# Turning the tail rows of K and Q, and the LayerNorm rows, by DMA transposes instead of TensorE products

## The chip, the cores and the metric

The kernel runs on one core of a Trainium2 chip. The metric is device time in microseconds of one execution, lower is better. "Span" is the time from the first to the last instruction of one profiled execution.

## What is computed

The reference is the forward and backward pass of a small transformer block; all inputs are bf16, and it returns the output and eleven gradients. What matters here is the forward attention, which is recurrent over segments of 32 tokens:

```python
mem = mem0                                   # 8 rows of width 512
for s in range(64):                          # 2048 tokens in segments of 32
    xs = h[:, s*32:(s+1)*32, :]              # h = layernorm(x) * (1 + ca) + sa
    hcat = concat([mem, xs])                 # 40 rows
    q, k, v = hcat @ Wq, hcat @ Wk, hcat @ Wv    # 32 heads of width 128
    p = softmax(where(mask, q @ k.T * scale, -1e9))
    o = (p @ v) @ Wo                         # 40 x 512
    mem = o[:8]                              # carried to the next segment
    out.append(o[8:])
```

After it come the gated feed-forward block and then the gradients of everything.

## The kernel before

The phases run one after the other. The forward attention (`phase2`) takes about the first 960 us of the span. It loops over 64 steps, one for each segment. Four steps make a group, since 4 x 32 = 128 rows of x are one tile; I call them first to fourth step (`s4` = 0 to 3 in the code).

**The rows of a step.** Of the 40 rows of a segment only the 8 memory rows depend on the step before. The kernel splits them as 32 + 8: `hT` holds, as columns, the 8 memory rows and the first 24 rows of x, and the last 8 rows of x of all four segments of a group (the tail rows, tile `hb`) are projected together, one group ahead, in pieces that fill TensorE where a step has to wait. K and Q of the tail rows are collected as rows in the tiles `RBk` and `RBq` and must be turned into columns, `b_colsk` and `b_colsq` (two buffers each), from which GpSimd copies eight columns per head into the tiles `kT` and `qT` at the end of every step (`tails_in`).

**One step on TensorE** goes: K's and Q's projections of the 32 rows (`pass_ps`, L257); V's projection in three pieces (L659), between them the turning of K's and Q's rows (`turn_ps`, L829); the scores (`st_ps`, L839), which ScalarE takes through Exp into `ET` (one buffer, L841); the denominators (`or_ps`, L845) and the products with V (`or_ps`, L865); VectorE inverts the denominators (`rden`, L850) and scales into `Ost` (one buffer, L889; ScalarE does a third of it at L886); `Ost` is turned (`tps`, L857) and copied into `OT` (one buffer); the output projection (`at_ps`, L223); its folding (`at_ft`), from which the next step's memory columns come.

**Where the changed work stands.** In the third step, behind the products with V, TensorE turns K's tail rows in eight products (`turn_b`, L623); in the fourth step it does the same with Q's. They stand just ahead of the turning of `Ost`. After the output projection ScalarE and VectorE each copy one half out of PSUM (`evac_turned`). In the fourth step, ahead of the last products with V, TensorE turns the LayerNorm rows `h1` of the tile two groups ahead (`turn` of `p1_tile`, four products into `p1tp`, L420); ScalarE copies them to `hx`, and GpSimd copies the tail columns from `hx` to `hb`.

**SP's queue.** SP issues nearly all DMAs of the loop in program order. For each step: K's and Q's rows to DRAM (`KST`, `QST`, L594 and L595), a DMA transpose `VTr<-Vst` (L954) and a DMA transpose `Pst<-ET` (L962), each of 128 x 1408 values, that is 11 blocks of 128 x 128, then the stores of `Ost` (`OSR`, L997) and `OT` (L1010), and in the next step those of `VTr` (`VT`, L1040) and `Pst` (`PS`, L1041). Ahead of the last one GpSimd multiplies `Pst` by the inverted denominators (`norm`, L1038). At the end of the second and third steps the tail rows go out too, in six DMAs (L599, L602). GpSimd issues the copies of V's tail rows (`Vst<-RBv`, L794) and some small stores.

**What sets the order.** The order of every engine is the order of the program: `pin` adds a dependency from each instruction of the loop to the one before it on its engine. Waits between engines come from the tile framework, by tiles and buffers.

Of the kernel before, what the change touches and what calls it, by code (L numbers as in the profile page):

```python
# [9 lines left out]
AF = mybir.ActivationFunctionType  # L10
# [30 lines left out]
class K:  # L41
# [334 lines left out]
    def phase1_setup(self, ctx, psum_tile_fn):  # L376
        nc, tc, cfg, io = self.nc, self.tc, self.cfg, self.io
        D, DC, NT = cfg.D, cfg.DC, cfg.NT
        x_rows = io["A_x"].rearrange("o s d -> (o s) d")
        p1 = ctx.enter_context(tc.tile_pool(name="p1", bufs=1))  # L380
        p1w = ctx.enter_context(tc.tile_pool(name="p1w", bufs=2))
        ca1_bc = self.ca1_bc = p1.tile([128, D], F32, name="ca1_bc")
        sa_bc = self.sa_bc = p1.tile([128, D], F32, name="sa_bc")
        mhalf = p1.tile([128, 1], F32, name="mhalf1")
        nc.gpsimd.memset(mhalf[:], -0.5)
        nseg = 128 // cfg.T

        def p1_tile(j):

            st = {}  # L390

            def load():
                st["x0"] = p1w.tile([128, D], BF16, name="x0_1", bufs=1)
                nc.sync.dma_start(st["x0"][:], x_rows[j * 128:(j + 1) * 128, :])

            def stats():
                bs = p1w.tile([128, 6], F32, name="st1")
                nc.vector.bn_stats(bs[:], st["x0"][:])
                mv = p1w.tile([128, 2], F32, name="mv1")
                nc.vector.bn_aggr(mv[:], bs[:])  # L400
                ve = p1w.tile([128, 1], F32, name="ve1")
                nc.vector.tensor_scalar_add(ve[:], mv[:, 1:2], EPS)
                rstd = p1w.tile([128, 1], F32, name="rstd1")
                nc.gpsimd.tensor_tensor(rstd[:], ve[:], mhalf[:], op=ALU.pow)
                st.update(mv=mv, rstd=rstd)

            def scale():
                xh = st["xh"] = p1w.tile([128, D], F32, name="xh", bufs=1)
                nc.vector.tensor_scalar(xh[:], st["x0"][:], st["mv"][:, 0:1], st["rstd"][:, 0:1], op0=ALU.subtract, op1=ALU.mult)
                nc.vector.tensor_tensor(xh[:], xh[:], ca1_bc[:], op=ALU.mult)  # L410

            def shift():
                h1 = st["h1"] = p1w.tile([128, D], BF16, name="h1", bufs=1)
                nc.vector.tensor_tensor(h1[:], st["xh"][:], sa_bc[:], op=ALU.add)
                nc.gpsimd.dma_start(self.H1ROWS[j * 128:(j + 1) * 128, :], h1[:])

            def turn():
                tp = psum_tile_fn()
                for c in range(DC):
                    nc.tensor.transpose(tp[:, c, :], st["h1"][:, c * 128:(c + 1) * 128], self.ident[:])  # L420
                hx = p1w.tile([128, DC, 128], BF16, name="hx", bufs=3)
                nc.scalar.activation(hx[:], tp[:, 0:DC, :], AF.Copy)
                hb = p1w.tile([128, DC, nseg, 8], BF16, name="hb", bufs=2)
                nc.gpsimd.tensor_copy(hb[:], hx[:].rearrange("p c (s t) -> p c s t", t=cfg.T)[:, :, :, 24:cfg.T])
                return hx, hb

            return load, stats, scale, shift, turn

        return p1_tile

# [8 lines left out]
    def phase2(self):  # L439
        nc, tc, cfg, io = self.nc, self.tc, self.cfg, self.io  # L440
        D, DC, H, E, L, M, T, G, NS = cfg.D, cfg.DC, cfg.H, cfg.E, cfg.L, cfg.M, cfg.T, cfg.G, cfg.NS
# [13 lines left out]
        with ExitStack() as ctx:  # L455
# [38 lines left out]
            P1_AHEAD = 2  # L494
            NT = cfg.NT
            nseg_t = 128 // T
            hxs = {}

            def p1(j, k=None):
                if j < NT:  # L500
                    if j not in p1s:
                        p1s[j] = p1_tile(j)
                    for i in (range(1, 5) if k is None else [k]):
                        r = p1s[j][i]()
                        if r is not None:
                            hxs[j] = r
# [101 lines left out]
            def b_pieces(t):  # L608

                bt = btails[t] = {}  # L610
                RBt = RB

                def proj_b(x, a, n, eng):
                    hb = hxs[t][1]
                    self.col_pass(psp, Ws[x], 0, lambda c: hb[:, c, :, :].rearrange("p s q -> p (s q)"), RBt[x], eng, steps=(a, n))
                    if a + n == 8:
                        rows_out(RBt[x], DR[x], t * nseg_t, nseg_t)

                def turn_b(x):
                    bt[x] = btp.tile([128, 8, 128], BF16, name="b_cols" + x)  # L620
                    tp = psp.tile([128, 8, 128], BF16, name="turn_ps", tag="p")
                    for i in range(8):
                        nc.tensor.transpose(tp[:, i, :], RBt[x][:, i * 128:(i + 1) * 128], self.ident[:, :])  # L623

                    def f():
                        for hf in range(2):
                            self.evac(("act", "dve")[hf], bt[x][:, 4 * hf:4 * hf + 4, :], tp[:, 4 * hf:4 * hf + 4, :])

                    evacs.append(f)

                P = lambda x, a, n, eng: (lambda: proj_b(x, a, n, eng))
                T_ = lambda x: (lambda: turn_b(x))
                return {(0, "f1"): [P("k", 0, 4, "dve")], (1, "f1"): [P("k", 4, 4, "dve")], (1, "f2"): [P("q", 0, 2, "act")],
                        (2, "turn"): [T_("k")], (2, "f1"): [P("q", 2, 4, "dve")], (2, "f2"): [P("q", 6, 2, "act")],
                        (3, "turn"): [T_("q")]}

            evacs = []

            def evac_turned():
                while evacs:  # L640
                    evacs.pop(0)()

            first = b_pieces(0)
            firsts = {x: [first[k][0] for k in ks] + [evac_turned]
                      for x, ks in (("k", ((0, "f1"), (1, "f1"), (2, "turn"))),
                                    ("q", ((1, "f2"), (2, "f1"), (2, "f2"), (3, "turn"))))}
            slots = {}

            VCH = ((0, 4), (4, 4), (8, 3))
# [20 lines left out]
            def hb_rows(t):  # L670
                return lambda c: hxs[t][1][:, c, :, :].rearrange("p s q -> p (s q)")
# [10 lines left out]
            def v_chunk(s, k):  # L682

                t, s4 = s // nseg_t, s % nseg_t
                a, n = VCH[k]
                tails_of = VTAILS.get((s4, k), ()) if t + 1 < NT else ()
                ps = psp.tile([128, 512], F32, name="pass_ps", tag="p")
                hT = get_ht(s)
                for c in range(DC):
                    for j in range(3):  # L690
                        v_mm(ps, j, c, hT[:, c, :], j, a, n)
                    for of in tails_of:
                        v_mm(ps, 3, c, hb_rows(t + 1)(c), *of)
                if k > 0:
                    v_evac(("dve", "act")[k - 1], Vsts[s % 2], ps, a, n)
                for hl, ta, tn, o in tails_of:
                    self.evac(("act", "dve")[k], RBv[(t + 1) % 2][32 * hl:32 * hl + 32, ta * E:(ta + tn) * E],
                              ps[96:128, o * E:(o + tn) * E])
                if k == 0:
                    v_evac("dve", Vsts[s % 2], ps, a, n)  # L700

            def fill(s4, where):
                for f in slots.pop((s4, where), []):
                    f()
# [81 lines left out]
            def tails_in(xs, s):  # L786
                for x in xs:
                    to_heads("pool", XT[x], btails[s // nseg_t][x][:], 0, 8, 8, 8 * (s % nseg_t))
# [15 lines left out]
            for s in range(NS):  # L804
                s4 = s % nseg_t
# [124 lines left out]
                    v_tails(0)  # L930
                if s == NS - 1:
                    first_tile[4]()
                v_chunk(s, 0)
                turns()
                v_chunk(s, 1)
# [30 lines left out]
                ost(0, or0, "dve")  # L966
                ost(1, or1, "act")
                den(2, or2)
                if s4 == 3:
                    p1(s // nseg_t + P1_AHEAD, 4)  # L970
                early = s4 == 0 and len(self.later) > 1
                if early:
                    self.pop_later()
# [3 lines left out]
                pv(2, or2)  # L977
                recip(2, 3, or2)
                ost(2, or2, "dve")
                fill(s4, "turn")  # L980
                if s == NS - 1:
                    turn_v(2)
                if more and s4 < 2:
# [21 lines left out]
                    first_tile[6]()  # L1005
                if s + 1 < NS:
                    tails_in("kq", s + 1)
                parts = self.split_pair(sb2, at_ps, "at")
                tail.collect(s4, [OT])
                nc.sync.dma_start(self.OT[s], gl3(OT))  # L1010
# [15 lines left out]
                if s + 1 in mod_at:  # L1026
                    load, products = self.mod_rest(psp, sb2, mod_at.index(s + 1))
# [1371 lines left out]
```

## Time and profile before

| what | value |
|---|---|
| median of 3 runs | 3001.38 us (2998.03, 3001.38, 3002.90) |
| span of the profiled execution | 2991.0 us, 105890 instructions |
| mean granted TensorE clock | 0.996 |
| DMA engines busy, mean GB/s | 0.86 and 216 over one group of the loop, 400.00 to 457.15 us |
| DMA traffic of the whole run | 703.05 MB, of it 486.09 MB on SP's queue |

Of the profiled execution the page gives only its span; the median of the runs is 10.4 us more, which is taken for what lies around it. In the views, PE is TensorE, PEld its weight loads, DVE VectorE, ACT ScalarE, POOL GpSimd and SP the engine whose queue issues most DMAs. A row of a timeline gives start, duration, engine, line, operation, output and input tiles and, in brackets, how long the engine was idle before it and what ended that. Matmuls are pipelined: the duration of one includes its way through the array, and several overlap, so rows are compared by their starts. A row of the table by windows gives busy time by engine with the number of instructions, then the granted clock, the mean busy share of the 16 DMA engines (packets are counted where they start, and may overlap, so that it can be above 1) and GB/s.

### The profile page before, as it was taken

The numbers are of one execution on the slowest core, as the hardware profiler recorded it, in microseconds if no ns is written. First come the engines' busy times: TensorE is split into PE (matmuls) and PEld (weight loads), VectorE is DVE, ScalarE is ACT, GpSimd is POOL, SyncE is SP. The second block draws the span as 40 slices with busy tenths as digits, with TensorE's granted clock in tenths as the row PEclk, the third lists the DMA queues.
The fourth block names the chain that finished last, engine by engine and source line by source line (L and its number), as shares of the span: only waits on it lengthen the run. The fifth ranks groups of instructions, "written<-read, shape, count | busy, mean of one in ns | idle before, by whom it ended". The sixth has DMA issues, their size and how long they took to land.

```text
span 2991.0 us, 105890 instructions
## 1 busy us (share of the span) xinstructions
PE 2932.8 (98%) x43975; PEld 1839.9 (62%) x44049; DVE 1612.4 (54%) x3679; ACT 1271.8 (43%) x3057; POOL 1197.2 (40%) x2456
## 2 busy tenths in 40 slices
PE   6999999999999999999999999999999999999999
PEld 3666666666665544445677777777777754445454
DVE  5566656666655788833456665566566532222230
ACT  2555555555555533312355555555555520011111
POOL 2454555555545222221344444444444422333321
PEclk8999999999999999999999999999999999999999
DMA  9898888889889899998699999999999997766574
GB/s 310 222 223 211 214 217 217 213 214 215 217 218 277 211 230 226 229 290 278 200 251 251 251 253 243 250 250 250 255 255 250 254 281 245 242 207 214 178 245 144
DMA packets 836438, 703.05 MB, mean 235 GB/s; under 512 B 536643, under 2 KB 708851, under 8 KB 835061
## 3 DMA queue, kind: packets, MB, share of 16 engines
q1 hardware_dynamic: 710756, 486.09, 65.5%
q0 software_dynamic: 54640, 148.90, 15.7%
q10 hardware_dynamic: 70560, 61.28, 6.5%
q8 instruction: 347, 5.69, 0.8%
q14 instruction: 135, 1.10, 0.1%
HBM read 294.99 MB, written 276.35 MB: 191 GB/s over the span
## 4 chain that ended last, share of the span: by engine, by line
PE 87%; issue 5%; DMA 3%; DVE 2%; POOL 1%; ACT 1%; SPq 1%; DVEq 0%; POOLq 0%; ACTq 0%
PE pass_ps L257 14%; PE gps L2180 9%; PE dh_ps L215 8%; PE pass_ps L659 5%; PE g_ps L1810 5%; PE gps5o L2195 4%; PE dhq_ps L223 4%; PE at_ps L223 4%; PE mm L1291 3%; PE dh_tps L215 3%; PE gps L1470 3%; PE turn_ps L829 2%; PE mm L1266 2%; PE mm L1251 1%; PE tps L1727 1%
## 5 line engine op out<-in xcount | busy, mean ns | idle before, releaser
L2180 PE MATMUL gps<-rows,hrows 128*128 128x512 bf16 (+2 forms) x2125 | 415.6, 355 | 1.8
L2180 PEld LDWEIGHTS <-hrows 128*128 128x128 bf16 x2160 | 211.3, 98 | 204.5
L61 ACT ACTIVATE ot<-gps 128x512 bf16<-128x512 f32 (+3 forms) x75 | 41.3, 550 | 362.2 <-PE gps L2180 229.1
L1855 POOL COPY dOst<-RAd 96x512 bf16<-96x512 bf16 x128 | 75.3, 613 | 297.8 <-DVE RAd L63 297.8
L1038 POOL TENSOR_TENSOR Pst<-Pst,rden 120x1408 bf16<-120x1408 bf16 x63 | 159.9, 2538 | 77.8 <-issue 49.6
L659 PE MATMUL pass_ps<-Wv,hT 128*32 128x512 bf16 (+2 forms) x2304 | 187.2, 358 | 0.0
L63 DVE CAST ot<-gps 128x512 bf16<-128x512 f32 (+3 forms) x76 | 48.1, 633 | 247.0 <-PE gps L2180 169.9
L2184 POOL DMA_DIRECT2D out_dram<-ot x108 | 81.5, 755 | 249.1 <-DVE ot L63 141.9
L257 PEld LDWEIGHTS <-hT 128*32 128x32 bf16 x4096 | 114.8, 97 | 103.9 <-issue 5.7
L63 DVE CAST Vst<-pass_ps 96x512 bf16<-96x512 f32 x128 | 87.3, 682 | 107.0 <-ACT RBv L61 98.5
L215 PE MATMUL dh_ps<-WvT,dVT 128*32 128x512 bf16 x2048 | 133.3, 380 | 1.7
L659 PE MATMUL pass_ps<-Wv,hb 128*32 128x512 bf16 (+2 forms) x636 | 128.7, 353 | 0.0
L257 PE MATMUL pass_ps<-Wq,hT 128*32 128x512 bf16 x2048 | 123.9, 383 | 4.8 <-DMA Wq<-in_A_Wq_dram 4.8
L257 PE MATMUL pass_ps<-Wk,hT 128*32 128x512 bf16 x2048 | 123.2, 382 | 2.5 <-POOL hT L549 1.1
L223 PE MATMUL at_ps<-Wo,OT 128*32 128x256 bf16 x4096 | 123.9, 273 | 0.7 <-DMA Wo<-in_A_Wo_dram 0.6
L257 PE MATMUL pass_ps<-WoT,dyT 128*32 128x256 bf16 (+1 forms) x3072 | 122.5, 308 | 0.9 <-ACT dyT L1936 0.9
L223 PE MATMUL dhq_ps<-WqT,dQT 128*32 128x256 bf16 x4096 | 122.9, 273 | 0.0
L215 PE MATMUL dh_ps<-WkT,dKT 128*32 128x512 bf16 x2048 | 122.3, 380 | 0.0
L794 POOL DMA_DIRECT2D Vst<-RBv x192 | 99.9, 526 | 55.6 <-ACT ET L841 34.4
L2195 PE MATMUL gps5o<-WoT,rows 128*128 128x512 bf16 x548 | 120.6, 379 | 1.0 <-DMA rows<-OSR 0.4
L223 PEld LDWEIGHTS <-dQT 128*32 128x32 bf16 x4096 | 109.7, 97 | 15.8
L315 DVE TENSOR_TENSOR dST<-dh_ps,dST 128x512 bf16<-128x512 f32 x64 | 44.3, 692 | 129.9 <-ACT dST L314 129.9
(471 smaller groups left out, 6991.2 us busy)
## 6 DMA issues: line engine op xcount, KB each, us to landing
OSR<-Ost SPq DMA_DIRECT2D x64, 352.0 KB
OT<-OT SPq DMA_DIRECT2D x64, 352.0 KB
PS<-Pst SPq DMA_DIRECT2D x64, 352.0 KB
Pst_l<-PS SPq DMA_DIRECT2D x64, 352.0 KB
OT_l<-OT SPq DMA_DIRECT2D x64, 352.0 KB
DVR<-rows_x POOLq DMA_DIRECT2D x64, 352.0 KB, 6.3
DKR<-rows_x POOLq DMA_DIRECT2D x64, 352.0 KB, 5.7
DQR<-rows_x POOLq DMA_DIRECT2D x64, 352.0 KB, 3.4
```

What stands on the lines that cost most here:

```text
L63: return nc.vector.tensor_copy(out, in_)
L215: self.nc.tensor.matmul(ps[32 * j:32 * j + 32, :], lhsT=lhsT, rhs=w, start=(n < 4), stop=(n >= total - 4), tile_position=(0, 32 * j))
L223: nc.tensor.matmul(ps[32 * j:32 * j + 32, :], lhsT=x[k], rhs=w[k][:, 256 * d:256 * d + 256], start=(n == 0), stop=(n == total - 1), tile_p ...
L257: self.nc.tensor.matmul(ps[32 * j:32 * j + 32, :], lhsT=lhs(c), rhs=rhs, start=(c == 0), stop=(c == DC - 1), tile_position=(0, 32 * j))
L659: nc.tensor.matmul(ps[32 * j:32 * j + 32, o * E:(o + n) * E], lhsT=lhsT, rhs=wc[:, 3 * a + hl:3 * (a + n - 1) + hl + 1:3, :], start=(c == ...
L794: nc.gpsimd.dma_start(Vst[96 + 8 * j:104 + 8 * j, :], rb[32 * j + o:32 * j + o + 8, :])
L1038: nc.gpsimd.tensor_tensor(Pst[0:120, :, :], Pst[0:120, :, :], rden[:, :].unsqueeze(2).to_broadcast([120, G, 128]), op=ALU.mult)
L1291: nc.tensor.matmul(hp[:], lhsT=xT[:, fc, :], rhs=wT[:, fc, :], start=(n == 0), stop=(n == 2 * FC - 1))
L1470: nc.tensor.matmul(ps[:], lhsT=h2r[:, j, c * 128:(c + 1) * 128], rhs=xr[:, j, :], start=(j == 0), stop=(j == NT - 1))
L1810: nc.tensor.matmul(ps[:, j, 0:w], lhsT=lh[:, g * GW:(g + 1) * GW], rhs=rh[:, g * GW:g * GW + w], start=True, stop=True)
L2180: nc.tensor.matmul(ps[:, 0:ng * E], lhsT=hrows[:, tp_, c * 128:(c + 1) * 128], rhs=rows[:, tp_, 0:ng * E], start=(tp_ == 0), stop=(tp_ == ...
L2195: nc.tensor.matmul(pss[gg][:], lhsT=rows[:, t, gg * E:(gg + 1) * E], rhs=dyrows[:, t, :], start=(n == 0), stop=(n == NTP - 1))
```

## The change

From the second group on (`t > 0`) K's and Q's tail rows are turned by one DMA transpose each (128 x 1024 values, eight blocks), issued by SP ahead of `VTr<-Vst` in the third and fourth steps, instead of eight products and two copies. From the third tile on (`j >= 2`) the LayerNorm rows are turned by one DMA transpose (128 x 512 values, four blocks), issued at the same place of the fourth step, instead of four products and a copy; GpSimd's copy of the tail columns moves behind the output projection (`ends`). The first group, and the first two tiles, stay as they were.

```diff
             def turn():
-                tp = psum_tile_fn()
-                for c in range(DC):
-                    nc.tensor.transpose(tp[:, c, :], st["h1"][:, c * 128:(c + 1) * 128], self.ident[:])
                 hx = p1w.tile([128, DC, 128], BF16, name="hx", bufs=3)
-                nc.scalar.activation(hx[:], tp[:, 0:DC, :], AF.Copy)
+                if j < 2:
+                    tp = psum_tile_fn()
+                    for c in range(DC):
+                        nc.tensor.transpose(tp[:, c, :], st["h1"][:, c * 128:(c + 1) * 128], self.ident[:])
+                    nc.scalar.activation(hx[:], tp[:, 0:DC, :], AF.Copy)
+                else:
+                    nc.sync.dma_start(hx[:], st["h1"][:], transpose=True)
                 hb = p1w.tile([128, DC, nseg, 8], BF16, name="hb", bufs=2)
-                nc.gpsimd.tensor_copy(hb[:], hx[:].rearrange("p c (s t) -> p c s t", t=cfg.T)[:, :, :, 24:cfg.T])
+                st.update(hx=hx, hb=hb)
+                if j < 2:
+                    ends()
                 return hx, hb
 
-            return load, stats, scale, shift, turn
+            def ends():
+                nc.gpsimd.tensor_copy(st["hb"][:], st["hx"][:].rearrange("p c (s t) -> p c s t", t=cfg.T)[:, :, :, 24:cfg.T])
+
+            return load, stats, scale, shift, turn, ends
...
                 def turn_b(x):
                     bt[x] = btp.tile([128, 8, 128], BF16, name="b_cols" + x)
+                    if t > 0:
+                        nc.sync.dma_start(bt[x][:], RBt[x][:, 0:1024], transpose=True)
+                        return
                     tp = psp.tile([128, 8, 128], BF16, name="turn_ps", tag="p")
...
-                        (2, "turn"): [T_("k")], (2, "f1"): [P("q", 2, 4, "dve")], (2, "f2"): [P("q", 6, 2, "act")],
-                        (3, "turn"): [T_("q")]}
+                        (2, "rows"): [T_("k")], (2, "f1"): [P("q", 2, 4, "dve")], (2, "f2"): [P("q", 6, 2, "act")],
+                        (3, "rows"): [T_("q")]}
...
                 if s == NS - 1:
                     first_tile[4]()
+                fill(s4, "rows")
+                if s4 == 3:
+                    p1(s // nseg_t + P1_AHEAD, 4)
                 v_chunk(s, 0)
                 turns()
...
                 den(2, or2)
-                if s4 == 3:
-                    p1(s // nseg_t + P1_AHEAD, 4)
...
                 ost(2, or2, "dve")
-                fill(s4, "turn")
...
                 if s + 1 < NS:
                     tails_in("kq", s + 1)
+                if s4 == 3:
+                    p1(s // nseg_t + P1_AHEAD, 5)
                 parts = self.split_pair(sb2, at_ps, "at")
```

More of the change, by code (lines that the diff above doesn't have):

```diff
@@ L644, in phase2 @@
             firsts = {x: [first[k][0] for k in ks] + [evac_turned]
-                      for x, ks in (("k", ((0, "f1"), (1, "f1"), (2, "turn"))),
-                                    ("q", ((1, "f2"), (2, "f1"), (2, "f2"), (3, "turn"))))}
+                      for x, ks in (("k", ((0, "f1"), (1, "f1"), (2, "rows"))),
+                                    ("q", ((1, "f2"), (2, "f1"), (2, "f2"), (3, "rows"))))}
             slots = {}
```

## The prediction

> **What bounds the kernel now.** I read the page, then the attention loop's stretch: one group of four steps in the engines' table, TensorE and VectorE by timeline, SP's queue, the waits.
>
> ```profile
> PE 2932.8 (98%) x43975; PEld 1839.9 (62%) x44049; DVE 1612.4 (54%) x3679; ACT 1271.8 (43%) x3057; POOL 1197.2 (40%) x2456
> ```
>
> ```profile
> core 0: us, PE busy (x) PEld busy (x) DVE busy (x) ACT busy (x) POOL busy (x), PEclk, DMA share, GB/s
> 404.00:406.00 2.00, 2.00 (x44) 1.04 (x40) 0.80 (x2) 0.52 (x2) 1.47 (x3) 1.00 1.01 393
> 456.50:461.30 4.80, 4.66 (x113) 3.50 (x115) 3.40 (x9) 1.78 (x6) 2.68 (x9) 1.00 1.19 150
> 400.00:457.15 57.15, 57.01 (x1136) 38.30 (x1135) 34.95 (x84) 33.12 (x89) 29.63 (x60) 1.00 0.86 216
> ```
>
> The last row is one group, 57.15 us: TensorE busy 57.01 at full clock, DMA engines 0.86. Two engines are near their limit and the change moves work from the first to the second. But the busy time of a pipelined matmul covers the wait of its successor, so 57.01 doesn't say that removed matmuls shorten the group. Ask what starts the next thing that cannot move. For the removed products it is the output projection (at_ps). Here is its approach in a third step (K's turn is there) and in the last group's third step, which has no tail rows and so no turn:
>
> ```profile
> 425.63 0.37 PE L845 MATMUL or_ps<-ones,ET 128*128 128x1 bf16 x8
> 426.65 0.33 PE L865 MATMUL or_ps<-Vst,ET 128*128 128x128 bf16 x3
> 426.81 0.61 PE L623 MATMUL turn_ps<-ident,RBk 128*128 128x128 bf16 x8
> 427.26 0.38 PE L857 MATMUL tps<-ident,Ost 120*128 120x120 bf16 x4
> 428.20 1.06 PE L223 MATMUL at_ps<-Wo,OT 128*32 128x256 bf16 x32
> ...
> 940.22 0.37 PE L845 MATMUL or_ps<-ones,ET 128*128 128x1 bf16 x8
> 941.74 0.38 PE L857 MATMUL tps<-ident,Ost 120*128 120x120 bf16 x4 [0.18 <-DVE Ost L889]
> 942.75 1.49 PE L223 MATMUL at_ps<-Wo,OT 128*32 128x256 bf16 x48
> ```
>
> From the denominators to at_ps it is 428.20 - 425.63 = 2.57 us with the turn and 942.75 - 940.22 = 2.53 without. VectorE shows why:
>
> ```profile
> 426.11 0.21 DVE L850 RECIPROCAL rden<-or_ps 120x8 f32<-120x8 f32 x1 [0.33 <-PE or_ps L845]
> 426.41 0.69 DVE L889 TENSOR_TENSOR Ost<-or_ps,rden 120x512 bf16<-120x512 f32 x1
> 427.02 0.18 DVE L850 RECIPROCAL rden<-or_ps 120x3 f32<-120x3 f32 x1
> 427.23 0.56 DVE L889 TENSOR_TENSOR Ost<-or_ps,rden 120x384 bf16<-120x384 f32 x1
> 427.73 0.41 DVE L63 COPY OT<-tps 128x480 bf16<-128x480 bf16 x1
> ```
>
> Five instructions back to back, then at_ps 0.06 us after the last. The turn (426.81 to 427.26) lies wholly under them.
>
> **What the change removes.** The instruction order shows 15 x 8 products for K, 15 x 8 for Q, 14 x 4 for LayerNorm, and their copies; otherwise TensorE, VectorE and ScalarE keep their order. The chain of work gives these products 0.45, 0.45 and 0.24 us, so 15 x 0.90 + 14 x 0.24 = 16.9 us of TensorE time. On the path is less:
> - K's turn: 2.57 - 2.53 = 0.04 us, 15 times: 0.6. Q's turn stands in the same place of the fourth step; I give it the same 0.6.
> - LayerNorm's four products stand ahead of the last or_ps products, for which the second reciprocal waits, so they delay VectorE's chain. A fourth step with them (439.84 to 442.62) takes 2.78 us; that of the last group but one, which has Q's turn but no LayerNorm products (897.53 to 900.07), 2.54. 14 x 0.24 = 3.4.
> - The copies (ScalarE 603 and VectorE 425 ns for K and for Q, ScalarE 615 for hx) lie ahead of at_hi, before which ScalarE still idles 0.68 us for at_ps in the fourth step: nothing on the path.
>
> Sum of gains: 0.6 + 0.6 + 3.4 = 4.6 us.
>
> **What it adds.** 44 transposes on SP, an in-order queue. No transpose of these sizes is in the trace; the nearest are those of 11 blocks:
>
> ```profile
> L954 SPq DMA_TRANSPOSE VTr<-Vst x63: 1281/1782/3419, 53.2 to 941.6; - x63
> L962 SPq DMA_TRANSPOSE Pst<-ET x63: 1288/1834/3164, 56.7 to 943.0; - x63
> ```
>
> Per block 0.12, 0.16 and 0.31 us. Eight blocks (K, Q) then hold SP for 0.9, 1.3 or 2.5 us, four (hx) for 0.5, 0.65 or 1.2, plus 0.1 between issues. I take the median rows, the same kind of instruction from the same queue. On the DMA engines the window 456.50:461.30, nearly all transposes, moved 150 GB/s at a share of 1.19, that is 126 GB/s of full engine time; plain rows (404:406) 393/1.01 = 389. The added 256 + 256 + 128 KB per group cost 655/126 = 5.2 us by the first and 1.7 by the second; I take 5.2. Idle in the group: 0.14 x 57.15 = 8.0. So the engines hold, at a share of about 0.95.
>
> [...]
>
> **Who waits.** SP around the two places:
>
> ```profile
> 426.10 0.43 SPq L595 DMA_DIRECT2D QST<-RA0q  x1
> 426.76 1.91 SPq L954 DMA_TRANSPOSE VTr<-Vst  x1
> 431.36 0.40 SPq L1010 DMA_DIRECT2D OT<-OT  x1
> 432.45 0.63 SPq L599 DMA_DIRECT2D QST<-RBq  x1
> ...
> 440.72 0.42 SPq L595 DMA_DIRECT2D QST<-RA1q  x1
> 441.37 1.70 SPq L954 DMA_TRANSPOSE VTr<-Vst  x1
> 443.17 1.86 SPq L962 DMA_TRANSPOSE Pst<-ET  x1
> ```
>
> K's transpose goes ahead of 426.76, where SP has hardly a gap: VTr, Pst, OSR and OT issue 1.4 us later. The gap before 432.45 (0.69 us) takes half back. In the fourth step Q's and hx's go ahead of 441.37: 1.3 + 0.65 + 0.2. So VTr, Pst, OSR and OT issue there 0.7 + 2.15 = 2.9 us late, up to 1.9 + 3.9 = 5.8 with the longest issues. Neither new transpose waits on fresh data: the rows and h1 are made in the step before. Who needs what is late:
> - ET has one buffer: the next step's Exp (ScalarE, 453.55) waits until Pst's transpose has read it. Before, it had landed at 448.25, when GpSimd's norm starts on it: 5.3 us of cover. Over the loop's fourth steps the same difference is 3.9 to 6.0.
> - Ost and OT, one buffer each, are stored behind Pst and rewritten at 455.3 and 456.9; issued at 445.1 and 446.5, a store of 352 KB takes 352 x 1.024/389 = 0.9 us, so they have over 5 us too.
> - norm (2.54 us) moves with Pst to about 451, and the PS store, K's and Q's row stores and VTr behind it on SP; SP's gaps before the PS store and VTr (1.6 and 1.5 us) and the wait of 3.9 us in the step after take it back. Row buffers are double.
> - GpSimd: the copies of Q's columns wait for Q's transpose and hb for hx's, with ao_tail, hT, norm and the three Vst stores queued behind. Their readers are the next step's scores (453) or later; GpSimd waited 2.5 us ahead of norm and 5.7 behind the Vst stores.
>
> So in most groups nothing late reaches TensorE. For the tightest boundaries (about 4 us of cover) I add 1 us in all. Forecast: 3001.4 - 4.6 + 1.0 = 2997.8. The profiled span is 2991.0, 10.4 below the median; I keep that difference for what lies around, so a span of 2987.4. Its own range is 2994 to 3003.
>
> **Rivals.**
> 1. All removed TensorE time comes out: 3001.4 - 16.9 = 2984.5. For: TensorE 57.01 of 57.15. Against: 2.57 against 2.53. It would need VectorE's chain to start earlier, and nothing ahead of it is removed.
> 2. Slower: Pst's transpose lands after the next Exp is ready, and TensorE waits for ET. It decides once SP and the DMA engines put it back more than 5.3 - 0.3 = 5.0 us; with the longest issues 5.8, so 0.8 per group, 15 x 0.8 = 12: 3001.4 - 4.6 + 12 = 3008.8, and 3016 where delays reach 6.3. For: the fourth step's SP has no gap from 432.45 on, and the share goes to 0.95. Against: needs maxima three times running.
> 3. The DMA engines become the bound: were the cost twice 5.2, 10.4 - 8.0 = 2.4 us per group are over, 15 x 2.4 = 36: 3033. Against: the window's rate already holds the transposes' stalls. [...]
>
> **How the numbers follow.** Forecast 0.60, rival 1 0.10, rival 2 0.25, rival 3 0.05. A measurement of this kernel can tell about 0.2%, 6 us: below 2995.4 is faster (rival 1 and 0.03 of the forecast's), above 3007.4 slower (rivals 2 and 3, but for 0.05 of rival 2 that stays below). So 0.13, 0.62, 0.25. The range of 8 in 10 leaves out rival 1, rival 3 and the upper end of rival 2: 2989 to 3014.
>
> **What would show it.** Right: denominators to at_ps stays near 2.53 in third and fourth steps; VTr in fourth steps issues 2 to 4 us later against the step; no wait of Exp on a DMA. Wrong: third steps shorter by 0.4 (rival 1); ScalarE or TensorE waiting on Pst<-ET, or groups over 57.15 (rival 2); a DMA share of 1 with SP late in every step (rival 3).

## The result and the profile after

The change made the kernel slower: 3045.55 us, the median of four runs (3041.03 to 3045.70), against 3002.14 us before, a ratio of 1.0154 with a 95% interval of 1.0141 to 1.0167. The forecast was 2997.8 us, with 2989 to 3014 as range.

Of every execution since the prediction both the time and the span are known, and the time is the span plus 1.7 to 2.2 us, mostly 1.8. So of the 10.4 us hardly 2 lie around the span. By that the profiled execution before took some 2992.8 us, 9.3 below the median; that after took 3041.0 us, 4.5 below its median. The two profiles differ by 48.2 us, of which 33.1 lie in 14 groups of the attention loop: from at_ps of the fourth step to at_ps of the 60th it was 800.85 us (99.22 to 900.07), and is 833.93. The rest is 3.8 ahead of that, 5.7 in the last four steps and 5.7 behind the loop. The same stretches outside the loop sum to between 2193 and 2210 us in the other variants (2190 before, 2205 after), so I explain only the loop's 33.1 us, 2.36 per group (57.20 to 59.57).

First the busy time on the page, then the loop in the table by windows:

```profile
PE 2940.0 (97%) x43679; PEld 1831.0 (60%) x43753; DVE 1596.9 (53%) x3649; ACT 1250.7 (41%) x3013; POOL 1193.7 (39%) x2456
```

```profile
core 0: us, PE busy (x) PEld busy (x) DVE busy (x) ACT busy (x) POOL busy (x), PEclk, DMA share, GB/s
103.04:936.97 833.93, 800.47 (x15552) 526.63 (x15550) 472.74 (x1125) 442.77 (x1191) 411.18 (x835) 0.99 0.91 217
```

TensorE is busy 800.47 of 833.93 us; before it was 797.23 of 800.85. So it now stands idle for 33 us instead of 4, with 275 matmuls less to do. The clock fell from 1.00 to 0.99. The DMA engines' share is 0.91, not 0.95, and no bound.

Now the approach to at_ps in TensorE's timeline, a third step and then a fourth:

```profile
442.85 0.37 PE L856 MATMUL or_ps<-ones,ET 128*128 128x1 bf16 x8
445.38 1.93 PE L223 MATMUL at_ps<-Wo,OT 128*32 128x256 bf16 x64
...
457.03 0.35 PE L856 MATMUL or_ps<-ones,ET 128*128 128x1 bf16 x8
459.60 1.60 PE L223 MATMUL at_ps<-Wo,OT 128*32 128x256 bf16 x52
```

From the denominators it is 2.53 and 2.57 us, where it was 2.57 and 2.78: this step of the prediction held (medians over 14 groups: 2.56 to 2.53 in third steps, 2.77 to 2.51 in fourth steps). TensorE waits elsewhere. The waits between 100 and 900 us (engine, line, tile waited for: us in total, times, longest):

```profile
POOL qT L65 <- DMA b_colsq<-RBq: 78.6, 14, 7.7
ACT ET L852 <- DMA Pst<-ET: 19.0, 12, 2.7
PE pass_ps L670 <- POOL hb L433: 14.2, 12, 2.2
PE or_ps L856 <- ACT ET L852: 10.8, 19, 1.8
```

14.2 + 10.8 = 25.0 us, where no wait of TensorE in the same groups before was longer than 0.7 us. Four of these waits were also followed by 3.4 us at half clock (last section), by estimate 1.7 us lost each (half of 3.4): 6.8. Together 31.8, nearly the 33.1. Where the lateness comes from is seen in SP's queue, here from a third step into a fourth:

```profile
271.72 1.46 SPq L976 DMA_TRANSPOSE Pst<-ET  x1
...
276.68 1.83 SPq L610 DMA_DIRECT2D QST<-RBq  x3
278.56 0.46 SPq L1053 DMA_DIRECT2D VT<-VTr  x1
279.13 0.36 SPq L1054 DMA_DIRECT2D PS<-Pst  x1
...
282.67 1.51 SPq L603 DMA_DIRECT2D QST<-RA1q  x1
284.23 1.27 SPq L630 DMA_TRANSPOSE b_colsq<-RBq  x1
285.55 1.27 SPq L425 DMA_TRANSPOSE hx<-h  x1
287.05 1.38 SPq L968 DMA_TRANSPOSE VTr<-Vst  x1
288.49 1.68 SPq L976 DMA_TRANSPOSE Pst<-ET  x1
...
293.48 0.44 SPq L1053 DMA_DIRECT2D VT<-VTr  x1
296.73 0.33 SPq L1054 DMA_DIRECT2D PS<-Pst  x1
```

at_ps of the fourth step starts at 278.95, yet Pst's transpose of that step is issued at 288.49, 9.5 us behind it; in the fourth step shown before it was 0.55 us (443.17 against 442.62). From one Pst to the next SP needs 16.77 us here, then 13.87, 11.85 and 17.19 (the next ones start at 302.36, 314.21, 331.40): 59.68 in a group. The only gap of size in these lines is that ahead of PS at 296.73: it waits for GpSimd's norm, which waits for Pst to land. In the timelines of TensorE and GpSimd, and in the chain that ended last, the same step looks so:

```profile
288.54 0.39 PE L670 MATMUL pass_ps<-Wv,hb 128*32 128x512 bf16 x1 [1.69 <-POOL hb L433]
294.76 0.25 PE L856 MATMUL or_ps<-ones,ET 128*128 128x1 bf16 x4 [1.76 <-ACT ET L852]
...
287.61 0.65 POOL L65 COPY qT<-b_colsq 128x192 bf16<-128x192 bf16 x3 [6.84 <-DMA b_colsq<-RBq]
288.19 0.29 POOL L433 COPY hb<-hx 128x128 bf16<-128x128 bf16 x1
294.17 2.53 POOL L1051 TENSOR_TENSOR Pst<-Pst,rden 120x1408 bf16<-120x1408 bf16 x1 [5.12 <-DMA Pst<-ET]
```

```profile
287.29 1.14 SPq L968
288.43 0.05 issue
288.49 5.55 DMA Pst<-ET
...
294.14 0.04 ACT ET L852
```

V's first piece waits for hb, the columns from the transpose at 285.55, which GpSimd copies only behind its copies of Q's columns; then Exp waits for Pst's transpose to have read ET, and TensorE for Exp. That is rival 2's mechanism, with a wait for hb ahead of it that no rival had.

What the new transposes cost SP, from the groups by tile (min/median/max ns); the third row is of an experiment below, with one block in the place of eight:

```profile
L630 SPq DMA_TRANSPOSE b_colsq<-RBq x15: 1268/1408/2872, 102.3 to 939.7; - x15
L425 SPq DMA_TRANSPOSE hx<-h x14: 1256/1310/2067, 104.7 to 883.6; - x14
```

```profile
L634 SPq DMA_TRANSPOSE x<-RBk x15: 1148/1164/2583, 86.4 to 899.7; - x15
```

One block 1.16 us, four 1.31, eight 1.41, and 11 (VTr, median) 1.84: the issue depends little on the size. The kernel before shows it too: behind the attention, its feed-forward phase turns tiles of 128 x 512 values, four blocks, by DMA transposes on SP:

```profile
L1197 SPq DMA_TRANSPOSE hdT<-h x14: 1201/1202/1226, 990.7 to 1238.7; - x14
```

Pst's issue stood behind its step's at_ps by -0.2, 0.0, 0.7 and 1.0 us in first to fourth steps before (medians over the same 14 groups), and stands behind it by 3.5, 2.3, 5.4 and 8.4 us after. It is 9.3 us in the fourth step of the first of these groups, and 5.5 to 9.5 in the others: the lateness is carried from step to step, and doesn't grow further once TensorE waits for it.

**SP's account of a group.** Summing SP's rows of the same 14 groups, and the gaps ahead of each, gives (us per group):

| kernel | issuing | small gaps | ahead of VTr | ahead of Pst | ahead of PS | group |
|---|---|---|---|---|---|---|
| before | 44.4 | 3.7 | 2.4 | 0.4 | 6.3 | 57.2 |
| after | 49.3 | 3.5 | 0.9 | 0.3 | 5.5 | 59.6 |
| kq_only | 48.6 | 3.5 | 1.0 | 0.3 | 5.4 | 58.7 |
| spare1 | 47.6 | 3.5 | 1.0 | 0.3 | 5.6 | 58.0 |
| rb_pool | 42.9 | 3.4 | 1.0 | 0.3 | 12.5 | 60.1 |
| ps_late | 49.8 | 3.6 | 1.5 | 2.1 | 0.7 | 57.7 |
| ps_late_before | 41.4 | 6.6 | 6.3 | 2.6 | 0.4 | 57.1 |
| ps_late_kq | 48.4 | 3.6 | 2.2 | 2.2 | 0.6 | 57.1 |

Before, SP stood idle ahead of VTr for data that TensorE's step makes: 2.4 us, of which 0.9 (4 x 0.23, the gap that it always has) are no wait, so 1.5 us of room. After, that room is gone, and the 5.5 us ahead of PS stay. The issuing is no fixed price: the issues of the kernel before take 44.4 us, and 41.4 in ps_late_before, which moves one of them.

### The profile page after: what moved, and what is told of

Read it like the earlier page. It is cut to its first block, busy times and chain, and to the rows that moved or that the text cites. A ratio compares the mean times of both kernels' runs of the same rounds, so it can differ in the third digit from the quotient of the medians.

```text
span 3039.2 us, 105140 instructions
## 1 busy us (share of the span) xinstructions
PE 2940.0 (97%) x43679; PEld 1831.0 (60%) x43753; DVE 1596.9 (53%) x3649; ACT 1250.7 (41%) x3013; POOL 1193.7 (39%) x2456
## 4 chain that ended last, share of the span: by engine, by line
PE 80%; DMA 7%; issue 5%; DVE 3%; ACT 2%; SPq 2%; POOL 1%; DVEq 0%; POOLq 0%; ACTq 0%
PE pass_ps L257 12%; PE gps L2193 9%; PE dh_ps L215 8%; PE g_ps L1823 5%; PE pass_ps L670 4%; PE gps5o L2208 4%; PE dhq_ps L223 4%; PE at_ps L223 4%; PE mm L1304 3%; PE dh_tps L215 3%; PE gps L1483 3%; DMA Pst<-ET 2%; PE mm L1264 2%; PE turn_ps L840 2%; PE mm L1279 2%
## 5 line engine op out<-in xcount | busy, mean ns | idle before, releaser
L670 PE MATMUL pass_ps<-Wv,hb 128*32 128x512 bf16 (+2 forms) x636 | 128.6, 349 | 14.2 <-POOL hb L433 14.2
L223 PEld LDWEIGHTS <-OT 128*32 128x32 bf16 x4096 | 105.3, 98 | 17.4 <-DVE OT L63 4.3
```

The source lines that it names most:

```text
L223: nc.tensor.matmul(ps[32 * j:32 * j + 32, :], lhsT=x[k], rhs=w[k][:, 256 * d:256 * d + 256], start=(n == 0), stop=(n == total - 1), tile_p ...
L670: nc.tensor.matmul(ps[32 * j:32 * j + 32, o * E:(o + n) * E], lhsT=lhsT, rhs=wc[:, 3 * a + hl:3 * (a + n - 1) + hl + 1:3, :], start=(c == ...
```

## The experiments

The theory that I set out with was that SP's late queue delays Pst and the columns. Its rivals: the DMA engines' load, or the columns for hb alone. All ratios are against the kernel before on the same chip; a group is the mean of the same 14. It is read from one profiled execution, which took 9.3 us less than the median in the kernel before and up to 8.3 more (ps_pool); that is up to 0.6 us a group, so small differences in the last column tell little.

| kernel | median us | ratio, 95% | group us |
|---|---|---|---|
| kq_only | 3021.85 | 1.0079 [1.0062, 1.0095] | 58.67 |
| hx_only | 3002.59 | 1.0023 [1.0013, 1.0032] | 57.06 |
| spare8 | 3017.10 | 1.0064 [1.0041, 1.0087] | 58.46 |
| spare1 | 3009.61 | 1.0044 [1.0028, 1.0059] | 57.95 |
| rb_pool | 3044.66 | 1.0156 [1.0141, 1.0172] | 60.06 |
| rb_pool_before | 3001.16 | 1.0008 [0.9998, 1.0018] | 57.27 |
| ps_pool | 3020.64 | 1.0079 [1.0056, 1.0102] | 58.37 |
| early | 3034.69 | 1.0119 [1.0101, 1.0137] | 59.75 |
| ps_late | 3008.55 | 1.0039 [1.0026, 1.0052] | 57.71 |
| ps_mid | 3013.22 | 1.0050 [1.0036, 1.0064] | 58.10 |
| ps_late_before | 3001.47 | 1.0009 [1.0000, 1.0018] | 57.11 |
| ps_late_hx | 2997.13 | 0.9998 [0.9989, 1.0007] | 57.06 |
| ps_late_kq | 3000.38 | 1.0013 [1.0005, 1.0022] | 57.12 |
| ps_late_early | 3026.64 | 1.0094 [1.0072, 1.0116] | 58.78 |
| ps_late_kq_spare | 3007.69 | 1.0045 [1.0028, 1.0062] | 57.54 |
| ps_late_swap | 3011.45 | 1.0040 [1.0026, 1.0055] | 58.07 |

**Which part costs: kq_only and hx_only.** One part of the change each. In kq_only `turn` of the LayerNorm rows is as before, in hx_only `turn_b` and its place.

```diff
 kq_only:
-                if j < 2:
+                if True:
...
 hx_only:
-                    if t > 0:
-                        nc.sync.dma_start(bt[x][:], RBt[x][:, 0:1024], transpose=True)
-                        return
...
```

> Only K's and Q's tail rows are turned by DMA; the LayerNorm rows stay on TensorE. Queue theory (SP's in-order round sets the pace: Pst's transpose, its landing, norm, the PS store, the row stores, the next transposes; a transpose costs its issue on SP, about 1.4 us with either size, and before there were about 1.9 us per group to spare): 2 x 1.5 - 1.9 = 1.1 us per group, 15 groups, about +15 to +20 us, near 3019. Engine theory (the bytes on the DMA engines cost): 512 of 640 KB, four fifths of +43, near 3036. Wait theory (TensorE loses only where it waits for Q's columns or for hb): hb no longer comes by DMA, so that most of the +43 goes, below 3010.

> Only the LayerNorm rows are turned by DMA; K's and Q's tail rows stay on TensorE. Queue theory: 1.4 us of issue is within the 1.9 us to spare, and the 0.24 us per group gained on TensorE shows: -3 us, near 2999. Engine theory: 128 of 640 KB, a fifth of +43, about +9, near 3011. Wait theory: hb still waits for its transpose and the first V piece of the next step for hb, so about the 14 to 20 us which TensorE waited for hb: near 3018.

K and Q alone cost 24.7 us over the kernel before on that chip, the LayerNorm rows alone 5.4, both 43. It is no sum: the first issue fits into the room that SP has (1.5 us a group), what comes on top is paid. In hx_only's profile the 14 groups take 798.8 us, 2.1 less than before, so its excess lies outside the loop; why stays open.

**Is it the use of the columns, or the issue? spare8 and spare1.** The kernel before, with K's and Q's transposes added at the changed kernel's places into a tile that nobody reads; TensorE still turns them. spare8 turns eight blocks, spare1 one.

```diff
+                def spare(x):
+                    if t > 0:
...
+                        nc.sync.dma_start(sp, RBt[x][:, 0:1024], transpose=True)   # spare1: 0:128
...
-                        (3, "turn"): [T_("q")]}
+                        (3, "turn"): [T_("q")],
+                        (2, "rows"): [lambda: spare("k")], (3, "rows"): [lambda: spare("q")]}
```

> The kernel before, and on top of it K's and Q's tail rows are transposed by DMA (eight blocks each, at the places of the change) into a spare tile that nobody reads; TensorE still turns them. Queue theory: as with K and Q alone, without the TensorE gain of 1 us: near 3020. Engine theory: near 3037. Wait theory: nobody waits for the new data, so no change, 3002.

> As the run with spare transposes of eight blocks, but of one block each (128 x 128): an eighth of the bytes, as many issues. Queue theory: the issue is about as long whatever the size, so the same as with eight blocks, near 3020. Engine theory: an eighth of that run's excess, near 3006. Wait theory: 3002.

Two transposes that nobody reads cost 1.3 us a group, and with an eighth of the blocks still 0.75: the issue is the larger part. Neither theory's figure was met: spare1's 3009.61 us lie between the 3006 and the 3020 that I had expected, and the intervals of spare8 and spare1 overlap, so what the other blocks cost isn't resolved. SP's account gives both: spare8's two issues (medians 1.45 and 1.28 us) with a gap of 0.05 each are 2.8, spare1's (1.16 each) 2.4; less the 1.5 of room, that leaves 1.3 and 0.9.

**Is it the sum of SP's issues? rb_pool and rb_pool_before.** The six stores of the tail rows by GpSimd instead of SP, in the changed kernel and in the one before.

```diff
-                    nc.sync.dma_start(dram[s0:s0 + 4, 96 + 8 * j:104 + 8 * j, 0:8, :]...
+                    nc.gpsimd.dma_start(dram[s0:s0 + 4, 96 + 8 * j:104 + 8 * j, 0:8, :]...
...
```

> The changed kernel, with the stores of the tail rows (RBk, RBq: 12 DMAs in a group) issued by GpSimd instead of SP; every byte is moved as before. Queue theory: 12 issues of 0.58 to 0.65 us, 7.8 us with the gaps, leave SP's round of 59.7 us per group, TensorE sets the pace again at about 57, and some 14.75 x 2.7 = 40 us come back: near 3005, VTr's issue waiting for its data again. Engine theory (the DMA engines' time): no change, near 3045. Wait theory: the new data come a little earlier, 3030 to 3045.

> The kernel before, with the stores of the tail rows issued by GpSimd instead of SP. Queue theory: TensorE sets the pace there, so freeing SP by 7.8 us per group gains only the few stalls, 0 to -5 us, 2993 to 2999 beside 2997 to 3002 for the kernel before. Engine and wait theory: no change. If GpSimd's issues delay norm, up to +5.

My expectation for rb_pool fell. SP issues 6.4 us less per group, and the gap ahead of PS grows by 7.0. On SP those stores had run while Pst landed and norm worked, so their time cost nothing, and without them SP only waits longer for norm; on GpSimd they stand ahead of norm, which in 6 of the 14 second steps now starts without idle time before it. rb_pool_before shows no change that can be told (1.0008). From this I sharpened the theory of a **round** that kq_only's expectation names: Pst's issue, its landing, norm, the PS store, K's and Q's row stores, the new transposes, VTr and Pst again follow one another, since SP is in order and PS stands ahead of the rest (in the rows above, SP waits 2.8 us ahead of PS, 296.73, and issues K's row store only behind it, at 297.15). What is issued between PS and Pst lies in the round, what is issued behind Pst runs beside its landing.

**Shorten the round: ps_pool.** The PS store by GpSimd, right behind norm.

```diff
-                    nc.sync.dma_start(self.PS[s], Pst[:])
+                    nc.gpsimd.dma_start(self.PS[s], Pst[:])
```

> The changed kernel, with the store of Pst issued by GpSimd right behind norm instead of by SP, so that SP's queue no longer waits for norm (1.3 us per step in the changed kernel's trace) nor issues that store (0.4). Queue theory: 4 x 1.7 = 6.8 us per group leave the round, near 3005; up to 3015 if the store through GpSimd lands so late that the next Pst transpose waits for it. Engine theory: no change, near 3045. Wait theory: 3035 to 3045.

It took back half of the loss, less than the 3005 to 3015 that I had expected. SP doesn't wait for norm any more, but Pst (one buffer) now waits for the landing of that store: the gap ahead of it is 2.7 us a group, in place of the 5.5 ahead of PS. K's and Q's transposes are also longer in issue, 2.06 and 1.68 us in the median instead of 1.41; what keeps the other half isn't shown.

**Issue the late columns earlier: early.** Q's and the LayerNorm rows' transposes at the end of the third step.

```diff
-                        (3, "rows"): [T_("q")]}
+                        (2, "f3"): [T_("q")]}
...
-                if s4 == 3:
-                    p1(s // nseg_t + P1_AHEAD, 4)
...
                 fill(s4, "f2")
+                fill(s4, "f3")
+                if s4 == 2:
+                    p1(s // nseg_t + P1_AHEAD, 4)
```

> The changed kernel, with Q's and the LayerNorm rows' transposes issued at the end of the third step, behind the stores of Q's tail rows, instead of in the fourth. Queue theory: as many issues in the round, so the group stays near 59.7 us, 3035 to 3050. Engine theory: the same, 3045. Wait theory: GpSimd no longer stands waiting for Q's columns and hb's copy is in time, so the TensorE waits for hb go, 14 to 35 us: 3010 to 3030.

```profile
PE or_ps L856 <- ACT ET L852: 24.3, 28, 3.4
```

The waits for hb are gone, and those for ET are 24.3 us instead of 10.8: what waits changed, the round hardly did. Its ratio is lower than the changed kernel's (1.0119 against 1.0154, and the intervals don't overlap), so about a quarter of the loss may have hung on hb. The wait for hb is mostly a sign of the lateness, not its cause.

**Take the row stores out of the round: ps_late, ps_mid, ps_late_before, ps_late_hx.** The test of the round: nothing is added or taken away, SP only issues the PS store later, just ahead of the new transposes (in ps_mid between K's and Q's row stores).

```diff
                     nc.sync.dma_start(self.VT[s], VTr[:])
-                    nc.sync.dma_start(self.PS[s], Pst[:])
+                    ps_rows.append((s, Pst))
...
+                for r, rows in ps_rows:
+                    nc.sync.dma_start(self.PS[r], rows[:])
+                ps_rows.clear()
                 fill(s4, "rows")
```

> The changed kernel with one move: SP issues the store of Pst's rows (PS) not at the start of the next step but behind that step's K and Q row stores, just ahead of the new transposes, VTr and Pst. Nothing is left out and nothing is added to any queue. Round theory (Pst's transpose, its landing, norm, the PS store, the row stores, the new transposes, VTr and Pst again follow one another on an in-order queue, and that round sets the group): the row stores, some 3 us of every step, now run beside the landing and norm, so the legs are 4.8 + 2.5 + 0.4 + (1.4 or 2.7) + 1.9 = 11 to 12.4 us a step, under TensorE's 14.3. TensorE bounds again: a group of 57.0 to 57.6 us, 2994 to 3006 us. Theory that SP's time or the DMA engines' time as such is used up: both do just as much as before the move, so 59.5 us a group and 3040 to 3050. A third outcome, that Pst's transpose then waits for the landing of the PS store: 58 to 59 us, 3012 to 3030.

> The changed kernel, with the PS store between K's row stores and Q's: half of the row stores leave the round. Round theory: some 1.5 us shorter a step, so the legs sum to about 11.3 + 15.5 + 15.5 + 11.1 = 53.4 us if nothing else waits, under TensorE's 57.2; mostly bound by TensorE, 57.2 to 58.2 us, 2996 to 3017. Theory of SP's or the DMA engines' total time: 3040 to 3050.

> The kernel before the change with the same move of the PS store. Round theory: its group is already set by TensorE, the round had about 1.6 us to spare, so no gain: 57.1 to 57.4 us a group, 2994 to 3004 us, ratio 0.998 to 1.002. If the round also cost the kernel before something, down to 2985.

> Only the LayerNorm rows turned by DMA, K and Q by TensorE, with the same move of the PS store. Round theory with my sum of gains: the round is out of the way, and of the changed kernel's gain the LayerNorm part stays, 14 x 0.24 = 3.4 us: 2990 to 2998, a group of about 57.0 us. If that gain was none, 2996 to 3004.

One store moved in the queue brings the changed kernel from 1.0154 to 1.0039, three quarters of the loss, with all the same transposes, bytes and issues. ps_mid, half of the move, comes to 1.0050, not told apart from ps_late. The kernel before gains nothing from the move (TensorE bound it), though SP's gap ahead of VTr grows there from 2.4 to 6.3 us a group: the move makes room, and only a full queue needs it. SP in ps_late, the same steps as above:

```profile
261.21 1.77 SPq L979 DMA_TRANSPOSE Pst<-ET  x1
...
271.46 0.44 SPq L603 DMA_DIRECT2D QST<-RA1q  x1
271.99 0.39 SPq L945 DMA_DIRECT2D PS<-Pst  x1
272.42 1.59 SPq L630 DMA_TRANSPOSE b_colsq<-RBq  x1
274.06 1.35 SPq L425 DMA_TRANSPOSE hx<-h  x1
275.65 2.45 SPq L971 DMA_TRANSPOSE VTr<-Vst  x1
278.19 1.67 SPq L979 DMA_TRANSPOSE Pst<-ET  x1
```

PS goes out with a gap of 0.09, since norm was done in the shadow of the row stores, and Pst follows at_ps (271.93) by 6.3 us instead of 9.5. It did a little worse than I expected (2994 to 3006). There is a new wait, Pst for the landing of PS: the gap ahead of Pst is 2.1 us a group where 0.3 were before. But the gap is 2.2 and 2.6 us in ps_late_kq and ps_late_before, whose ratios are 1.0013 and 1.0009, so it is not the reason by itself.

**The last 11 us: ps_late_kq, ps_late_early, ps_late_kq_spare, ps_late_swap.** All with the moved store. Either hb is still late, or SP's issues in the fourth step are still too many. ps_late_kq leaves hx's transpose out; ps_late_early is ps_late with the edit of early; ps_late_kq_spare is ps_late_kq with a transpose of the LayerNorm rows that nobody reads; ps_late_swap issues hx ahead of Q and copies hb first.

```diff
 ps_late_kq_spare:
...
+                    nc.sync.dma_start(sp, st["h1"][:], transpose=True)
...
 ps_late_swap:
-                fill(s4, "rows")
                 if s4 == 3:
                     p1(s // nseg_t + P1_AHEAD, 4)
+                fill(s4, "rows")
...
```

> K's and Q's tail rows turned by DMA, the LayerNorm rows by TensorE as before, with the move of the PS store. Late-columns theory: hb is early as in the kernel before, so no wait of TensorE for it, 57.2 to 57.4 us a group, 2996 to 3003. If the rest comes from K's and Q's transposes on SP: about 57.7, 3004 to 3010.

> The changed kernel with both moves: the PS store just ahead of VTr's place, and Q's and the LayerNorm rows' transposes issued at the end of the third step instead of ahead of VTr in the fourth. With the PS store moved alone 11 us over the kernel before remained, and TensorE waited 7 times for hb at V's first piece (4.6 us) and twice for ET (2.2 us), each followed by 3.4 us of half clock in some cases. Late-columns theory: the rest is the wait for hb, which hangs on hx's and Q's transposes being issued some 10 us into the fourth step; issued a step earlier the waits go, 57.1 to 57.4 us a group, 2993 to 3002 us, ratio 0.998 to 1.002. Round theory alone (the rest is what the transposes' issue still costs on SP): 3004 to 3012, waits for ET in the place of those for hb.

> As the kernel with K and Q by DMA, LayerNorm rows by TensorE and the PS store moved (57.17 us a group, ratio 1.0013), plus a transpose of the LayerNorm rows in the changed kernel's place whose result nobody reads; hb still comes from TensorE's products. SP's queue carries what it carries in the changed kernel with the moved store. If the last 11 us come from hb being late for V's first piece: no loss, 57.1 to 57.3 us a group, 2994 to 3003. If they come from both transposes' issue in one step on SP, with Pst late behind it: 57.5 to 57.9 us, 3002 to 3012, TensorE waiting for ET.

> The changed kernel with the PS store moved, the LayerNorm rows' transpose issued ahead of Q's instead of behind it, and GpSimd's copy to hb ahead of its copies of K's and Q's columns. SP carries the same. If the last 11 us come from hb being late: hb comes 1.4 us earlier and no longer behind qT's wait for Q's columns, 57.2 to 57.5 us, 2995 to 3004. If from the issue sum on SP: 57.5 to 57.9 us, 3003 to 3012 as without the swap.

Without hx's transpose the loss is 1.0013; with one whose result nobody reads it is 1.0045, as much as the whole change with the moved store. Swapping the order left it at 1.0040, with the waits for hb down to 0.6 us and those for ET at 8.0:

```profile
PE or_ps L856 <- ACT ET L852: 8.0, 13, 2.0
```

In ps_late's own trace TensorE waits 6 times for hb, 3.2 us, and 4 times for ET, 2.4 us (the expectation of ps_late_early gives other counts). So the last part is SP's issue too, not hb. ps_late_early, for which I had expected at most 3012, fits this: the two issues now stand ahead of the row stores and with them ahead of PS, which goes out later, and the gap ahead of Pst is 3.0 us a group instead of 2.1:

```profile
SPq L977 <- DMA PS<-Pst: 38.2, 34, 2.0
```

In ps_late that row has 24.9 us, 22 times. No version beats the kernel before by more than can be told apart; ps_late_hx equals it.

## Why the prediction was wrong

- **TensorE's gain: right where the products stood, not for the group.** The turns of K and Q lay under VectorE's chain. That removing them brings little is shown by ps_late_kq: 57.12 us a group with them gone and SP out of the way, against 57.11 of ps_late_before. For the LayerNorm products I had 0.24 us a group. In hx_only the fourth step from the denominators to at_ps is 0.22 us shorter (medians 2.77 and 2.55), but hx_only's and ps_late_hx's groups are only 0.14 and 0.05 shorter than those of the kernels without it, below what can be told; where the rest went isn't shown.
- **Lateness that SP "takes back": the step that failed.** I counted three idle stretches of SP as room: 1.6 us ahead of PS, 1.5 ahead of VTr, and 3.9 in the next step ahead of PS. Those ahead of PS are no room: PS waits for norm, norm for Pst's landing, and Pst was just issued late, so that wait moves along with the lateness (6.3 us a group before, 5.5 after). Only VTr's wait is for something that TensorE's step sets, 1.5 us a group in all. I had let 0.7 us of lateness pass from the third step into the fourth, and had it all taken back behind that; against the kernel before, third steps are 4.7 us late, fourth steps 7.4, and first and second steps still 3.7 and 2.3. The 2.9 us that I put under a cover of 5.3 were 7.4, so Exp waits and holds the step back. ps_late, in which the wait for norm is gone, shows it: Pst's issue stands 4.0, 1.5, 3.4 and 7.0 us behind at_ps there, and 3.3, 0.8, 2.7 and 5.0 in ps_late_kq, which lost next to nothing.
- **The price of an issue: mis-sized.** By blocks I had 1.3, 1.3 and 0.65 us. Medians are 1.41, 1.41 and 1.31, means 1.54, 1.64 and 1.40, 4.6 us a group instead of 3.25. I wrote that no transpose of these sizes is in the trace before; for four blocks this was wrong, and those of the feed-forward phase (1.20 us, shown above) would have given the price. SP's issuing as a whole grew by 4.9. Less the room of 1.5 and the shorter gap ahead of PS (0.8) it is 2.6; the group grew by 2.4.
- **Who reads the columns: wrong.** I said that the readers of b_colsq and hb are the next step's scores or later. hb is read by V's first piece of the next step, some 3 us sooner, and GpSimd's copies of Q's columns, ahead of hb in its queue, waited 78.6 us for the transpose. It cost 14.2 us of the waits, but with it out of the way (early, ps_late_swap) about the same time was waited for ET: it wasn't the bound, though about a quarter of the loss may have hung on it (early).
- **DMA engines: right in the outcome.** Share 0.91, no bound; their time in a group went from 0.88 x 57.20 = 50.3 to 0.91 x 59.57 = 54.2 us, 3.9 more where I had 5.2. spare1 moved an eighth of spare8's blocks and still cost some two thirds of it.
- **Rival 2** had the right mechanism but I took it to need the longest issues together, and priced it at 3009 to 3016 us; it happens with the median ones, group after group, and half-clock stretches come on top.

## What to carry to other kernels

Of an in-order DMA queue, ask of every gap what it waits for: a gap that ends with something the queue itself started moves along with a delay and is no room (here that ahead of PS, 6.3 us a group before and 5.5 after). Add up a whole period, issues and gaps, and take as room only waits for work that another engine paces. And where a queue is full, look first for a store that stands in it waiting for its data, ahead of work that is ready: moving that one store was worth some 34 us in the changed kernel, and nothing in the kernel before, where TensorE set the pace.

## What was not expected of the hardware

- The issue of an SBUF to SBUF transpose takes SP 1.16, 1.31, 1.41 and 1.84 us (medians) for 1, 4, 8 and 11 blocks of 128 x 128 (the first from spare1, the others from the changed kernel): eleven times the blocks take 1.6 times as long. The shortest of one block is 1.145 us (spare1). One size spreads too: four blocks take 1.20 us in the feed-forward phase of the kernel before and 1.74 in ps_late_kq_spare (medians), and the single issues of eight in the changed kernel took 1.27 to 2.87.
- A wait of 1.3 to 2.2 us on TensorE can be followed by half its clock for 3.4 us: in the changed kernel's trace the windows 171.20:174.60, 475.00:478.40, 536.40:539.80 and 775.30:778.70 show a granted clock of 0.50 to 0.51, behind waits of 2.16, 1.27, 1.69 and 1.67 us that ended up to 2 us ahead. Six other waits in the loop, of 1.2 to 2.1 us, were not followed by it. The four stretches last 3.41 us each and begin at 171.18, 474.96, 536.40 and 775.34, that is 89, 18 and 70 times 3.413 us apart. TensorE's records leave 2.16, 1.48, 1.90 and 1.72 us idle in the 3.41 us ahead of them; but the wait of 2.08 us that ended at 410.20 had no half clock behind it, so what decides isn't shown.
